# Moving an attention kernel's leftover rows into 64-partition tiles, with earlier casts and a later request for batch 2

## The chip, the cores and the metric

The kernel runs on one core of a Trainium2 chip. The metric is the device time of one execution in microseconds. Ratios between kernels are computed from the mean time of one kernel's fast runs over the mean of the other's fast runs in the same rounds on the same chip, with a 95% interval; they are therefore not quite the ratio of the medians that are quoted beside them. PE is the matmul engine and PEld its weight loads, DVE the vector engine, ACT the scalar engine, POOL the GpSimd engine, SP the engine that only issues transfers.

## The reference

Attention without softmax over 8 batches, 8 heads, 576 rows, head width 64; then a dense block of 512 to 2048 to 512 over all 4608 rows:

```python
kv  = einsum('bhsd,bhse->bhde', k, v)
out = einsum('bhsd,bhde->bhse', q, kv)
out = out / sqrt(mean(out*out, -1) + 1e-6) * g_norm
x   = out.transpose(0, 2, 1, 3).reshape(4608, 512)
h   = x @ w_in
y   = (h * sigmoid(1.702 * h)) @ w_out
```

576 rows are 512 + 64. The kernel treats the first 512 rows of each head as four blocks of 128 and the last 64 as "rests". The rests of all batches are gathered into a ninth tile of the dense block.

## The kernel before

Heads are handled in pairs. For each pair, `kv` accumulates four 128-row matmuls and one matmul over the rests into PSUM, `q` transposes the q blocks, `out` multiplies, and `ss` and `apply` do the normalization. The rests of heads 0 to 3 lie in partitions 0 to 63 and those of heads 4 to 7 in partitions 64 to 127 of the same tile. The v rests stand in a tile of zeros, so that a matmul over all 128 partitions picks the right half:

```python
def load_rest(dst, n, b, g, eng):          # g: heads 0..3 or 4..7
    eng.dma_start(out=dst, in_=srcs[n][b, 4*g : 4*g+4, SM:S, :].rearrange("h p d -> p h d"))
...
for c in range(NPAIR):                     # first batch: k, q f32 on SP; v and rests cast on POOL's queue
    load_rows(first["k"][:, h0:h1, :], "k", 0, h0, h1, nc.sync)
    load_rows(vh0[:, h0:h1, :], "v", 0, h0, h1, nc.gpsimd)
    load_rows(first["q"][:, h0:h1, :], "q", 0, h0, h1, nc.sync)
    if c % 2 == 0:
        first_rests(c // 2)
... # weights, batch 1 and batch 2, all on POOL's queue

def kv(self, c, alone):
    ...
    for j in range(J):                     # L214
        nc.tensor.matmul(o, self.kh[:, c, j, :], self.vh[...], start=(j == 0), stop=False)
    nc.tensor.matmul(                      # L221: 128 rows, half of them zeros in vr
        t[:, c, :], self.kr[:, c % 2, :], self.vr[:, c, :], start=False, stop=True
    )
    ...
def q(self, c):
    for j in range(J):                     # L235
        nc.tensor.transpose(t[:, j*P : (j+1)*P], self.qh[:, c, j, :], ident)
    if c >= 2:                             # L237: two transposes for four pairs
        nc.tensor.transpose(t[:, SM : SM+P], self.qr[:, c-2, :], ident)
    ...
a0 = Attention(0)
for c in range(NPAIR):                     # the first batch
    casts(0, [c], False)
    if c:
        a0.ss(c - 1)
    a0.kv(c, True)
    a0.q(c)
    a0.out(c)
    if c:
        a0.apply(c - 1)
```

The dense block of tile t (`hT` is the hidden matmul, L302; `o` the projection, L342) has the attention of batch t + 1 woven into it. For tile 0 that is done in the projection, pair by pair as data comes; from tile 1 on, kv and q of the next batch each follow one of the hidden groups.

Of the kernel before, what the change touches and what calls it, by code (L numbers as in the profile page):

```python
# [8 lines left out]
F16 = mybir.dt.float16  # L9
F32 = mybir.dt.float32  # L10
# [3 lines left out]
P = 128  # L14
# [3 lines left out]
def kernel(  # L18
# [45 lines left out]
            out=dst, in_=srcs[n][b, h0:h1, 0:SM, :].rearrange("h (p j) d -> p h (j d)", j=J)  # L64
        )

    def load_rest(dst, n, b, g, eng):
        eng.dma_start(out=dst, in_=srcs[n][b, 4 * g : 4 * g + 4, SM:S, :].rearrange("h p d -> p h d"))

    def load_batch(b, parts, eng):  # L70
        tiles = {}
        for n in "kvq":
            tiles[n] = stage.tile([P, H, J * D], F32, name=f"{n}f", tag=f"{n}f")
            tiles[n + "r"] = stage.tile([P, 4, D], F32, name=f"{n}rf", tag=f"{n}rf")
        step = H // parts
        for h0 in range(0, H, step):
            for n in "kvq":
                load_rows(tiles[n][:, h0 : h0 + step, :], n, b, h0, h0 + step, eng)
            if h0 == 0:
                for n in "kvq":  # L80
                    for g in range(2):
                        load_rest(tiles[n + "r"][g * R : (g + 1) * R], n, b, g, eng)
        staged[b] = tiles

    def new_halves(b):
        t = [half.tile([P, NPAIR, J, P], F16, name=f"{n}h", tag=f"{n}h") for n in "kq"]
        t.append(half.tile([P, H, J * D], F16, name="vh", tag="vh"))
        t += [half.tile([P, 2, P], F16, name=f"{n}r", tag=f"{n}r") for n in "kq"]
        halves[b] = (*t, vrem[b % 2])
        return halves[b]  # L90

    kvb = [const.tile([P, NPAIR, P], F16, name=f"kvb{i}") for i in range(2)]
    vrem = [const.tile([P, NPAIR, P], F16, name=f"vrem{i}") for i in range(2)]
    ident = const.tile([P, P], F16)
    ones2 = const.tile([P, P], F16)
    eps_t = const.tile([P, 1], F32)
# [3 lines left out]
    w_out_sb = const.tile([P, FO, DM], F16)  # L100
    x_rem = const.tile([P, KO, B * R], F16)

    nc.vector.memset(vrem[0], 0.0)
    nc.vector.memset(eps_t, EPS)
    for t in kvb:
        nc.vector.memset(t, 0.0)
    nc.vector.memset(ones2, 0.0)
    nc.vector.memset(ones2[0:D, 0:D], 1.0)
    nc.vector.memset(ones2[D:P, D:P], 1.0)
    nc.vector.memset(vrem[1], 0.0)  # L110
    for hl in range(2):
        nc.scalar.dma_start(out=g_col[hl * D : (hl + 1) * D, :], in_=g_norm.unsqueeze(1))
    nc.scalar.preload_act_table_set("natural_log_exp_and_others")


    kh0, qh0, vh0, kr0, qr0, vr0 = new_halves(0)
    first = {n: stage.tile([P, H, J * D], F32, name=f"{n}f", tag=f"{n}f") for n in "kq"}
    staged[0] = first

    def as_heads(t):  # L120
        return t.rearrange("p u (l d) -> p (u l) d", l=2)

    def first_rests(g):
        r = slice(g * R, (g + 1) * R)
        load_rest(as_heads(kr0)[r], "k", 0, g, nc.gpsimd)
        load_rest(as_heads(vr0)[r, 4 * g : 4 * g + 4], "v", 0, g, nc.gpsimd)

    for c in range(NPAIR):
        h0, h1 = 2 * c, 2 * c + 2
        load_rows(first["k"][:, h0:h1, :], "k", 0, h0, h1, nc.sync)  # L130
        load_rows(vh0[:, h0:h1, :], "v", 0, h0, h1, nc.gpsimd)
        load_rows(first["q"][:, h0:h1, :], "q", 0, h0, h1, nc.sync)
        if c % 2 == 0:
            first_rests(c // 2)
        if c == 0:
            make_identity(nc, ident)
    for g in range(2):
        load_rest(as_heads(qr0)[g * R : (g + 1) * R], "q", 0, g, nc.gpsimd)
    gate_t = const.tile([P, 1], F32)
    nc.gpsimd.tensor_copy(gate_t, first["q"][:, H - 3, 0:1])  # L140


    for i in range(4):
        nc.gpsimd.dma_start(
            out=w_in_sb[:, :, i * SM : (i + 1) * SM],
            in_=moe_w_in[:, i * SM : (i + 1) * SM].rearrange("(ko ki) f -> ki ko f", ki=P),
        )
    for i in range(4):
        nc.gpsimd.dma_start(
            out=w_out_sb[:, 4 * i : 4 * i + 4, :],  # L150
            in_=moe_w_out[4 * i * P : 4 * (i + 1) * P, :].rearrange(
                "(fo ki) n -> ki fo n", ki=P
            ),
        )
    load_batch(1, 4, nc.gpsimd)
    load_batch(2, 1, nc.gpsimd)


    def casts(b, pairs, rest):
        if b not in halves:  # L160
            new_halves(b)
        src = staged[b]
        kh, qh, vh, kr, qr, vr = halves[b]

        def pair(dst, s, c):
            return dict(
                out=dst[:, c, :, :].rearrange("p j (l d) -> p j l d", l=2),
                in_=s[:, 2 * c : 2 * c + 2, :].rearrange("p l (j d) -> p j l d", j=J),
            )

        for c in pairs:
            nc.vector.tensor_copy(**pair(kh, src["k"], c))  # L172
            if b == 0:
                nc.scalar.copy(**pair(qh, src["q"], c))
                continue
            nc.vector.tensor_copy(
                out=vh[:, 2 * c : 2 * c + 2, :], in_=src["v"][:, 2 * c : 2 * c + 2, :]
            )
            if c == pairs[0] and rest:
                nc.vector.tensor_copy(  # L180
                    out=kr, in_=src["kr"].rearrange("p (u l) d -> p u (l d)", l=2)
                )
                for g in range(2):
                    rows = slice(g * R, (g + 1) * R)
                    nc.vector.tensor_copy(
                        out=vr[rows, 2 * g : 2 * g + 2, :],
                        in_=src["vr"][rows].rearrange("p (u l) d -> p u (l d)", l=2),
                    )
                nc.vector.tensor_copy(
                    out=qr, in_=src["qr"].rearrange("p (u l) d -> p u (l d)", l=2)  # L190
                )
            nc.vector.tensor_copy(**pair(qh, src["q"], c))


    xT = {}
# [1 line left out]
    class Attention:  # L197
# [9 lines left out]
        def kv(self, c, alone):  # L207
# [5 lines left out]
            for j in range(J):  # L213
# [5 lines left out]
                    stop=False,  # L219
                )  # L220
            nc.tensor.matmul(  # L221
                t[:, c, :], self.kr[:, c % 2, :], self.vr[:, c, :], start=False, stop=True
            )
            cs = slice(c, c + 1) if alone else slice(0, NPAIR)
            if alone or c == NPAIR - 1:
                for hl in range(2):
                    r = slice(hl * D, (hl + 1) * D)
                    nc.vector.tensor_copy(self.kb[r, cs, r], t[r, cs, r])  # L228

        def q(self, c):  # L230
            n = SM + (P if c >= 2 else 0)
            pool, tag = (ps_h, "hT") if self.b < 2 else (ps_a, "att")
            t = pool.tile([P, SM + P], F16, name="qTp", tag=tag)
            for j in range(J):
                nc.tensor.transpose(t[:, j * P : (j + 1) * P], self.qh[:, c, j, :], ident)  # L235
            if c >= 2:
                nc.tensor.transpose(t[:, SM : SM + P], self.qr[:, c - 2, :], ident)  # L237
            s = attn.tile([P, SM + P], F16, name="qT", tag="qT")
            nc.vector.tensor_copy(s[:, 0:n], t[:, 0:n])  # L239
            self.qT[c] = s  # L240

        def out(self, c):
# [10 lines left out]
            else:  # L253
                n = NPAIR * R
                for i in range(NPAIR):
                    nc.tensor.matmul(
                        t.rearrange("p c r -> p (c r)")[:, i * R : (i + 1) * R],
                        self.kb[:, i, :],
                        self.qT[i | 2][:, SM + (i // 2) * R : SM + (i // 2 + 1) * R],
                        start=True,  # L260
                        stop=True,
                    )
# [113 lines left out]


    a0 = Attention(0)
    for c in range(NPAIR):
        casts(0, [c], False)  # L380
        if c:
            a0.ss(c - 1)
        a0.kv(c, True)
        a0.q(c)
        a0.out(c)
        if c:
            a0.apply(c - 1)
    a0.ss(NPAIR - 1)
    a0.apply(NPAIR - 1)

    live = {0: a0}

# [3 lines left out]
    for t in range(NT):  # L396
# [6 lines left out]
        def at2(i, f, *args):  # L403
            u2.setdefault(i, []).append(lambda: f(*args))
# [3 lines left out]

        if t < 2:
            at1(5, of(t, "out", NPAIR))  # L410
            at2(2, of(t, "ss", NPAIR, True))
            at2(2, of(t, "apply", NPAIR))
        if t == 0:
            new_halves(1)
            start(1)
            for c in range(NPAIR):
                s0 = 22 + 10 * c
                at2(s0, casts, 1, [c], c == 0)
                at2(min(s0 + 7, 63), of(1, "kv", c, True))
                at2(min(s0 + 9, 63), of(1, "q", c))  # L420
                if c < NPAIR - 1:
                    at2(s0 + 15, of(1, "out", c))
                    at2(s0 + 19, of(1, "ss", c))
                    at2(s0 + 19, of(1, "apply", c))
            at2(63, load_batch, 3, 1, nc.sync)
        elif b < B:
            at1(2, casts, b, list(range(NPAIR)), True)
            at1(2, start, b)
            for c in range(NPAIR):
                at1(8 + c, of(b, "kv", c, False))  # L430
# [5 lines left out]
            if b + 2 < B:  # L436
                at2(2, load_batch, b + 2, 1, nc.sync)
        if t == 1:
            at1(("ko", 1), of(1, "out", NPAIR - 1))
            at1(("ko", 2), of(1, "ss", NPAIR - 1))  # L440
            at1(("ko", 3), of(1, "apply", NPAIR - 1))
        dense(t, u1, u2, 4 if t < 2 else 0, t == 0)

# [29 lines left out]
```

## Time and profile before

| | before |
|---|---|
| median of the runs | 321.68 us (321.29 to 323.17) |
| span of the profiled run | 320.4 us |
| PE busy | 289.5 us |
| first hidden matmul | 28.56 us |
| one steady batch (start of its hidden matmuls to the next) | 31.81 us |

The page's engine totals and its row of 40 slices, for PE in the kernel before. A digit is the busy tenth of a slice of 8 us:

```profile
PE 289.5 (90%) x1560; PEld 139.7 (44%) x1560; DVE 112.4 (35%) x260; ACT 176.4 (55%) x284; POOL 32.7 (10%) x52
...
PE   0167999769899999999999999999999999999993
```

PE is full from the twelfth slice on. Only the first 88 us hold idle time. What ended it, from the list of PE's waits in the kernel before (total us, times, longest):

```profile
PE kvp L214 <- DMA vh<-in_v_dram: 8.6, 1, 8.6
PE kvp L221 <- DMA kr<-in_k_dram: 6.1, 1, 6.1
PE outT L245 <- DVE qT L239: 4.4, 6, 1.0
PE ss L273 <- ACT sq L265: 2.7, 4, 0.7
PE hT L302 <- DVE qT L239: 1.5, 1, 1.5
PE hT L302 <- DVE xT L283: 1.4, 1, 1.4
```

The first two lines are the start: 8.6 us to the first v pair, then 6.1 us to the k rests. The others are chains between engines in the attention of batches 0 and 1.

From there on the batches follow each other evenly.

### The profile page before, as it was taken

The numbers are of one execution on the slowest core, as the hardware profiler recorded it, in microseconds if no ns is written. First come the engines' busy times: TensorE is split into PE (matmuls) and PEld (weight loads), VectorE is DVE, ScalarE is ACT, GpSimd is POOL, SyncE is SP. The second block draws the span as 40 slices with busy tenths as digits, with TensorE's granted clock in tenths as the row PEclk, the third lists the DMA queues.
The fourth block names the chain that finished last, engine by engine and source line by source line (L and its number), as shares of the span: only waits on it lengthen the run. The fifth ranks groups of instructions, "written<-read, shape, count | busy, mean of one in ns | idle before, by whom it ended". The sixth has DMA issues, their size and how long they took to land.

```text
span 320.4 us, 3978 instructions
## 1 busy us (share of the span) xinstructions
PE 289.5 (90%) x1560; PEld 139.7 (44%) x1560; DVE 112.4 (35%) x260; ACT 176.4 (55%) x284; POOL 32.7 (10%) x52
## 2 busy tenths in 40 slices
PE   0167999769899999999999999999999999999993
PEld 0033445325444554455445544554455444444441
DVE  2053017654346334633462356225622520020021
ACT  2067762466775667566756675667567756206500
POOL 8552395000000000000000000000000000000000
PEclk9999999999999999999999999999999999999998
DMA  6999979599901770267026702000300030003022
GB/s 147 220 205 194 250 234 349 186 373 321 302 0 82 245 248 0 100 235 240 2 115 227 236 0 122 11 0 0 133 0 2 0 131 1 2 0 132 2 65 67
DMA packets 37012, 41.49 MB, mean 130 GB/s; under 512 B 11200, under 2 KB 33728, under 8 KB 35968
## 3 DMA queue, kind: packets, MB, share of 16 engines
q1 hardware_dynamic: 27728, 29.23, 27.2%
q0 software_dynamic: 9104, 12.00, 16.8%
q8 instruction: 12, 0.20, 0.2%
q14 instruction: 8, 0.07, 0.1%
q10 hardware_dynamic: 160, 0.00, 0.0%
HBM read 36.70 MB, written 9.44 MB: 144 GB/s over the span
## 4 chain that ended last, share of the span: by engine, by line
PE 87%; ACT 4%; DMA 3%; DVE 2%; issue 1%; POOL 1%; DVEq 0%; POOLq 0%
PE hT L302 38%; PE o L342 37%; DMA kr<-in_k_dram 3%; PE ss L273 3%; PE outT L245 3%; PE kvp L214 2%; PE qTp L235 2%; DVE qT L239 1%; ACT ln L275 1%; ACT rs L277 1%; ACT sq L265 1%; POOL vh L63 1%; PE kvp L221 1%; PE hO L302 0%; ACT L270 0%
## 5 line engine op out<-in xcount | busy, mean ns | idle before, releaser
L342 PE MATMUL o<-w_out_sb,gT 128*128 128x512 f16 x576 | 137.0, 379 | 0.0
L311 ACT ACTIVATE gT<-hT 128x512 f16<-128x512 f32 x142 | 84.4, 598 | 75.9 <-PE hT L302 75.7
L302 PE MATMUL hT<-xT,w_in_sb 128*128 128x512 f16 x504 | 119.7, 381 | 3.0 <-DVE qT L239 1.5
L342 PEld LDWEIGHTS <-gT 128*128 128x128 f16 x576 | 55.3, 98 | 66.7 <-issue 5.4
L302 PEld LDWEIGHTS <-w_in_sb 128*128 128x128 f16 x576 | 54.8, 98 | 63.4 <-issue 7.2
L350 DVE COPY osb<-o 128x512 f32<-128x512 f32 x36 | 24.7, 685 | 62.1 <-PE o L342 62.1
L283 DVE SCALAR_TENSOR_TENSOR xT<-outT,g_col,rs 128x512 f16<-128x512 f32 x32 | 24.0, 750 | 50.0 <-ACT rs L277 50.0
L265 ACT ACTIVATE sq<-outT 128x512 f16<-128x512 f32 (+1 forms) x40 | 21.7, 544 | 27.3 <-PE outT L245 27.3
L275 ACT ACTIVATE ln<-ss,eps_t 128x512 f32<-128x512 f32 (+1 forms) x40 | 25.8, 645 | 17.1 <-PE ss L273 17.0
L228 DVE CAST kvb<-kvp 64x64 f16<-64x64 f32 (+1 forms) x28 | 8.6, 307 | 50.2 <-PE kvp L221 50.0
L277 ACT ACTIVATE rs<-ln 128x512 f32<-128x512 f32 (+1 forms) x40 | 23.5, 587 | 1.3
L214 PE MATMUL kvp<-vh,kh 128*128 128x128 f16 x128 | 13.3, 231 | 8.6 <-DMA vh<-in_v_dram 8.6
L239 DVE COPY qT<-qTp 128x512 f16<-128x512 f16 (+1 forms) x32 | 14.6, 457 | 13.8 <-PE qTp L237 8.2
L214 PEld LDWEIGHTS <-kh 128*128 128x128 f16 x128 | 10.3, 102 | 19.7 <-DVE kh L172 7.7
L273 PE MATMUL ss<-sq,ones 128*128 128x512 f16 (+1 forms) x40 | 15.1, 378 | 3.6 <-ACT sq L265 2.7
L245 PE MATMUL outT<-qT,kvb 128*128 128x512 f16 x32 | 12.9, 404 | 4.6 <-DVE qT L239 4.4
L172 DVE CAST kh<-kf 128x512 f16<-128x512 f32 x32 | 13.7, 429 | 1.1 <-DMA kf<-in_k_dram 1.1
L302 PE MATMUL hT<-x_rem,w_in_sb 128*128 128x512 f16 x64 | 14.0, 379 | 0.0
L235 PE MATMUL qTp<-ident,qh 128*128 128x128 f16 x128 | 13.4, 231 | 0.0
L235 PEld LDWEIGHTS <-qh 128*128 128x128 f16 x128 | 10.4, 104 | 6.6
L221 PE MATMUL kvp<-vrem,kr 128*128 128x128 f16 x32 | 7.3, 229 | 6.1 <-DMA kr<-in_k_dram 6.1
L287 DVE SCALAR_TENSOR_TENSOR x_rem<-outT,g_col,rs 128x256 f16<-128x256 f32 x8 | 3.9, 483 | 25.0 <-ACT rs L277 25.0
(44 smaller groups left out, 114.5 us busy)
## 6 DMA issues: line engine op xcount, KB each, us to landing
out_dram<-osb SPq DMA_DIRECT2D x8, 1024.0 KB, 3.8
kf<-in_k_dram SPq DMA_DIRECT2D x5, 1024.0 KB, 5.9
vf<-in_v_dram SPq DMA_DIRECT2D x5, 1024.0 KB, 8.5
qf<-in_q_dram SPq DMA_DIRECT2D x5, 1024.0 KB, 11.2
w_in_sb<-in_moe_w_in_dram POOLq DMA_DIRECT2D x4, 512.0 KB, 8.8
w_out_sb<-in_moe_w_out_dram POOLq DMA_DIRECT2D x4, 512.0 KB, 16.7
kf<-in_k_dram SPq DMA_DIRECT2D x4, 256.0 KB, 7.9
qf<-in_q_dram SPq DMA_DIRECT2D x4, 256.0 KB, 8.7
```

Source lines behind the costliest of these rows:

```text
L214: nc.tensor.matmul(o, self.kh[:, c, j, :], self.vh[:, 2 * c : 2 * c + 2, j * D : (j + 1) * D], start=(j == 0), stop=False,)
L235: nc.tensor.transpose(t[:, j * P : (j + 1) * P], self.qh[:, c, j, :], ident)
L245: nc.tensor.matmul(t.rearrange("p c r -> p (c r)"), self.kb[:, c, :], self.qT[c][:, 0:SM], start=True, stop=True,)
L265: nc.scalar.activation(sq[:, 0:n], t, AFT.Square)
L273: nc.tensor.matmul(t[:, 0:n], ones2, sq[:, 0:n], start=True, stop=True)
L275: nc.scalar.activation(ln[:, 0:n], t[:, 0:n], AFT.Ln, bias=eps_t, scale=1.0 / D)
L277: nc.scalar.activation(rs[:, 0:n], ln[:, 0:n], AFT.Exp, bias=0.0, scale=-0.5)
L283: nc.vector.scalar_tensor_tensor(self.x[:, c, :], o, g_col, rs, op0=ALU.mult, op1=ALU.mult)
L302: nc.tensor.matmul(h, w_in_sb[:, ko, fo * P : (fo + 1) * P], x[:, ko, :], start=(ko == 0), stop=(ko == KO - 1),)
L311: nc.scalar.activation(gT[:, fo, :], h, AFT.Gelu_apprx_sigmoid)
L342: nc.tensor.matmul(os[mo], gT[:, fo, mo * P : (mo + 1) * P], w_out_sb[:, fo, :], start=(fo == 0), stop=(fo == FO - 1),)
L350: nc.vector.tensor_copy(osb[:, mo, :], os[mo])
```

## The change

It moves all eight heads' rests of a tensor into one tile of 64 partitions, in one transfer in place of two. The zero-filled v tile goes, and so does the contraction over its zeros. First-batch v is no longer cast by the transfer. Casts run one pair ahead and are spread over DVE, ACT and POOL. Batch 1's attention is spread differently over the first projection, and batch 2 is requested on SP's queue once batch 1's third q pair is in. For batches 0 and 1 one multiplication by a mask replaces the two copies of `kv`. The diff, cut to its core:

```diff
-    def load_rest(dst, n, b, g, eng):
-        eng.dma_start(out=dst, in_=srcs[n][b, 4 * g : 4 * g + 4, SM:S, :].rearrange("h p d -> p h d"))
+    def load_rest(dst, n, b, eng):
+        eng.dma_start(out=dst, in_=srcs[n][b, :, SM:S, :].rearrange("h p d -> p h d"))
...
-        t += [half.tile([P, 2, P], F16, name=f"{n}r", tag=f"{n}r") for n in "kq"]
-        halves[b] = (*t, vrem[b % 2])
+        t += [half.tile([R, NPAIR, P], F16, name=f"{n}r", tag=f"{n}r") for n in "kqv"]
+        halves[b] = t
... (first batch: rests first on POOL's queue, then k, v, q pair by pair on SP's)
         for c in pairs:
+            h = slice(2 * c, 2 * c + 2)
             nc.vector.tensor_copy(**pair(kh, src["k"], c))
+            eng = nc.vector if b > 1 else nc.gpsimd
+            eng.tensor_copy(out=vh[:, h, :], in_=src["v"][:, h, :])
+            if b > 1 or (b == 0 and c % 2):
+                nc.vector.tensor_copy(**pair(qh, src["q"], c))
+            else:
                 nc.scalar.copy(**pair(qh, src["q"], c))
+    def cast_rests(b):
+        for n, t in (("kr", kr), ("vr", vr), ("qr", qr)):
+            nc.gpsimd.tensor_copy(out=t.rearrange("p c (l d) -> p (c l) d", l=2), in_=src[n])
...
             nc.tensor.matmul(
-                t[:, c, :], self.kr[:, c % 2, :], self.vr[:, c, :], start=False, stop=True
+                t[:, c, :], self.kr[:, c, :], self.vr[:, c, :], start=False, stop=True
             )
...
-            if c >= 2:
-                nc.tensor.transpose(t[:, SM : SM + P], self.qr[:, c - 2, :], ident)
+            nc.tensor.transpose(t[:, SM:S], self.qr[:, c, :], ident[0:R, 0:R])
...
+    casts(0, [0])
     for c in range(NPAIR):
-        casts(0, [c], False)
+        a0.kv(c, True)
+        a0.q(c)
         if c:
             a0.ss(c - 1)
-        a0.kv(c, True)
-        a0.q(c)
+        if c + 1 < NPAIR:
+            casts(0, [c + 1])
         a0.out(c)
...
+    def load_third():
+        nc.scalar.copy(after, staged[1]["q"][:, H - 3, 0:1])
+        nc.sync.dma_start(out=after[0:D, :], in_=g_norm.unsqueeze(1))
+        load_batch(2, 1, nc.sync)
...
-                s0 = 22 + 10 * c
-                at2(s0, casts, 1, [c], c == 0)
+                s0 = 30 + 7 * c
+                at2(s0, casts, 1, [c])
```

More of the change, by code (lines that the diff above doesn't have):

```diff
@@ L73, in load_batch @@
             tiles[n] = stage.tile([P, H, J * D], F32, name=f"{n}f", tag=f"{n}f")
-            tiles[n + "r"] = stage.tile([P, 4, D], F32, name=f"{n}rf", tag=f"{n}rf")
+            tiles[n + "r"] = stage.tile([R, H, D], F32, name=f"{n}rf", tag=f"{n}rf")
         step = H // parts
@@ L80, in load_batch @@
                 for n in "kvq":
-                    for g in range(2):
-                        load_rest(tiles[n + "r"][g * R : (g + 1) * R], n, b, g, eng)
+                    load_rest(tiles[n + "r"], n, b, eng)
         staged[b] = tiles
@@ L87, in new_halves @@
         t.append(half.tile([P, H, J * D], F16, name="vh", tag="vh"))
-        t += [half.tile([P, 2, P], F16, name=f"{n}r", tag=f"{n}r") for n in "kq"]
-        halves[b] = (*t, vrem[b % 2])
+        t += [half.tile([R, NPAIR, P], F16, name=f"{n}r", tag=f"{n}r") for n in "kqv"]
+        halves[b] = t
         return halves[b]
     kvb = [const.tile([P, NPAIR, P], F16, name=f"kvb{i}") for i in range(2)]
-    vrem = [const.tile([P, NPAIR, P], F16, name=f"vrem{i}") for i in range(2)]
     ident = const.tile([P, P], F16)
@@ L101 @@
     x_rem = const.tile([P, KO, B * R], F16)
-    nc.vector.memset(vrem[0], 0.0)
     nc.vector.memset(eps_t, EPS)
@@ L109, with load_w_in @@
     nc.vector.memset(ones2[D:P, D:P], 1.0)
-    nc.vector.memset(vrem[1], 0.0)
-    for hl in range(2):
-        nc.scalar.dma_start(out=g_col[hl * D : (hl + 1) * D, :], in_=g_norm.unsqueeze(1))
-    nc.scalar.preload_act_table_set("natural_log_exp_and_others")
-    kh0, qh0, vh0, kr0, qr0, vr0 = new_halves(0)
-    first = {n: stage.tile([P, H, J * D], F32, name=f"{n}f", tag=f"{n}f") for n in "kq"}
-    staged[0] = first
-    def as_heads(t):
-        return t.rearrange("p u (l d) -> p (u l) d", l=2)
-    def first_rests(g):
-        r = slice(g * R, (g + 1) * R)
-        load_rest(as_heads(kr0)[r], "k", 0, g, nc.gpsimd)
-        load_rest(as_heads(vr0)[r, 4 * g : 4 * g + 4], "v", 0, g, nc.gpsimd)
+    nc.scalar.preload_act_table_set("natural_log_exp_and_others")
+    first = {n: stage.tile([P, H, J * D], F32, name=f"{n}f", tag=f"{n}f") for n in "kvq"}
+    staged[0] = first
+    _, _, _, kr0, qr0, vr0 = new_halves(0)
+    for n, t in (("k", kr0), ("v", vr0), ("q", qr0)):
+        load_rest(t.rearrange("p c (l d) -> p (c l) d", l=2), n, 0, nc.gpsimd)
+    make_identity(nc, ident)
+    for hl in range(2):
+        nc.gpsimd.dma_start(out=g_col[hl * D : (hl + 1) * D, :], in_=g_norm.unsqueeze(1))
     for c in range(NPAIR):
         h0, h1 = 2 * c, 2 * c + 2
-        load_rows(first["k"][:, h0:h1, :], "k", 0, h0, h1, nc.sync)
-        load_rows(vh0[:, h0:h1, :], "v", 0, h0, h1, nc.gpsimd)
-        load_rows(first["q"][:, h0:h1, :], "q", 0, h0, h1, nc.sync)
-        if c % 2 == 0:
-            first_rests(c // 2)
-        if c == 0:
-            make_identity(nc, ident)
-    for g in range(2):
-        load_rest(as_heads(qr0)[g * R : (g + 1) * R], "q", 0, g, nc.gpsimd)
-    gate_t = const.tile([P, 1], F32)
-    nc.gpsimd.tensor_copy(gate_t, first["q"][:, H - 3, 0:1])
-    for i in range(4):
+        for n in "kvq":
+            load_rows(first[n][:, h0:h1, :], n, 0, h0, h1, nc.sync)
+    def load_w_in(i):
         nc.gpsimd.dma_start(
@@ L147, with load_w_out @@
         )
-    for i in range(4):
+    def load_w_out(i):
         nc.gpsimd.dma_start(
@@ L154, with casts @@
         )
-    load_batch(1, 4, nc.gpsimd)
-    load_batch(2, 1, nc.gpsimd)
-    def casts(b, pairs, rest):
+    def casts(b, pairs):
         if b not in halves:
@@ L171, in casts @@
         for c in pairs:
+            h = slice(2 * c, 2 * c + 2)
             nc.vector.tensor_copy(**pair(kh, src["k"], c))
-            if b == 0:
-                nc.scalar.copy(**pair(qh, src["q"], c))
-                continue
-            nc.vector.tensor_copy(
-                out=vh[:, 2 * c : 2 * c + 2, :], in_=src["v"][:, 2 * c : 2 * c + 2, :]
-            )
-            if c == pairs[0] and rest:
-                nc.vector.tensor_copy(
-                    out=kr, in_=src["kr"].rearrange("p (u l) d -> p u (l d)", l=2)
-                )
-                for g in range(2):
-                    rows = slice(g * R, (g + 1) * R)
-                    nc.vector.tensor_copy(
-                        out=vr[rows, 2 * g : 2 * g + 2, :],
-                        in_=src["vr"][rows].rearrange("p (u l) d -> p u (l d)", l=2),
-                    )
-                nc.vector.tensor_copy(
-                    out=qr, in_=src["qr"].rearrange("p (u l) d -> p u (l d)", l=2)
-                )
-            nc.vector.tensor_copy(**pair(qh, src["q"], c))
+            eng = nc.vector if b > 1 else nc.gpsimd
[3 more added lines that the diff above has]
+            else:
+                nc.scalar.copy(**pair(qh, src["q"], c))
+    def cast_rests(b):
+        src = staged[b]
+        _, _, _, kr, qr, vr = halves[b]
+        for n, t in (("kr", kr), ("vr", vr), ("qr", qr)):
+            nc.gpsimd.tensor_copy(out=t.rearrange("p c (l d) -> p (c l) d", l=2), in_=src[n])
     xT = {}
@@ L221, in kv @@
             nc.tensor.matmul(
-                t[:, c, :], self.kr[:, c % 2, :], self.vr[:, c, :], start=False, stop=True
+                t[:, c, :], self.kr[:, c, :], self.vr[:, c, :], start=False, stop=True
             )
-            cs = slice(c, c + 1) if alone else slice(0, NPAIR)
-            if alone or c == NPAIR - 1:
+            if alone:
+                nc.vector.tensor_mul(self.kb[:, c, :], t[:, c, :], ones2)
+            elif c == NPAIR - 1:
                 for hl in range(2):
                     r = slice(hl * D, (hl + 1) * D)
-                    nc.vector.tensor_copy(self.kb[r, cs, r], t[r, cs, r])
+                    nc.vector.tensor_copy(self.kb[r, :, r], t[r, :, r])
         def q(self, c):
-            n = SM + (P if c >= 2 else 0)
             pool, tag = (ps_h, "hT") if self.b < 2 else (ps_a, "att")
-            t = pool.tile([P, SM + P], F16, name="qTp", tag=tag)
+            t = pool.tile([P, S], F16, name="qTp", tag=tag)
             for j in range(J):
                 nc.tensor.transpose(t[:, j * P : (j + 1) * P], self.qh[:, c, j, :], ident)
-            if c >= 2:
-                nc.tensor.transpose(t[:, SM : SM + P], self.qr[:, c - 2, :], ident)
-            s = attn.tile([P, SM + P], F16, name="qT", tag="qT")
-            nc.vector.tensor_copy(s[:, 0:n], t[:, 0:n])
+            nc.tensor.transpose(t[:, SM:S], self.qr[:, c, :], ident[0:R, 0:R])
+            s = attn.tile([P, S], F16, name="qT", tag="qT", bufs=5)
+            nc.vector.tensor_copy(s, t)
             self.qT[c] = s
@@ L258, in out @@
                         self.kb[:, i, :],
-                        self.qT[i | 2][:, SM + (i // 2) * R : SM + (i // 2 + 1) * R],
+                        self.qT[i][:, SM:S],
                         start=True,
@@ L378 @@
     a0 = Attention(0)
+    casts(0, [0])
     for c in range(NPAIR):
-        casts(0, [c], False)
+        a0.kv(c, True)
+        a0.q(c)
         if c:
             a0.ss(c - 1)
-        a0.kv(c, True)
-        a0.q(c)
+        if c + 1 < NPAIR:
+            casts(0, [c + 1])
+        if c == 1:
+            load_w_in(0)
         a0.out(c)
@@ L389 @@
     a0.apply(NPAIR - 1)
+    for i in range(1, 4):
+        load_w_in(i)
+    for i in range(4):
+        load_w_out(i)
+    load_batch(1, 4, nc.gpsimd)
+    after = const.tile([P, 1], F32)
+    def load_third():
+        nc.scalar.copy(after, staged[1]["q"][:, H - 3, 0:1])
+        nc.sync.dma_start(out=after[0:D, :], in_=g_norm.unsqueeze(1))
+        load_batch(2, 1, nc.sync)
     live = {0: a0}
@@ L410 @@
             at1(5, of(t, "out", NPAIR))
-            at2(2, of(t, "ss", NPAIR, True))
-            at2(2, of(t, "apply", NPAIR))
+            at2(5, of(t, "ss", NPAIR, True))
+            at2(5, of(t, "apply", NPAIR))
         if t == 0:
@@ L416 @@
             for c in range(NPAIR):
-                s0 = 22 + 10 * c
-                at2(s0, casts, 1, [c], c == 0)
-                at2(min(s0 + 7, 63), of(1, "kv", c, True))
-                at2(min(s0 + 9, 63), of(1, "q", c))
+                s0 = 30 + 7 * c
+                at2(s0, casts, 1, [c])
+                if c == 2:
+                    at2(s0, load_third)
+                if c == 0:
+                    at2(s0, cast_rests, 1)
+                at2(s0 + 5, of(1, "kv", c, True))
+                at2(s0 + 6, of(1, "q", c))
+                at2(s0 + 12, of(1, "out", c))
                 if c < NPAIR - 1:
-                    at2(s0 + 15, of(1, "out", c))
-                    at2(s0 + 19, of(1, "ss", c))
-                    at2(s0 + 19, of(1, "apply", c))
+                    at2(s0 + 17, of(1, "ss", c))
+                    at2(s0 + 17, of(1, "apply", c))
             at2(63, load_batch, 3, 1, nc.sync)
         elif b < B:
-            at1(2, casts, b, list(range(NPAIR)), True)
+            at1(2, casts, b, list(range(NPAIR)))
+            at1(2, cast_rests, b)
             at1(2, start, b)
@@ L438 @@
         if t == 1:
-            at1(("ko", 1), of(1, "out", NPAIR - 1))
-            at1(("ko", 2), of(1, "ss", NPAIR - 1))
+            at1(("ko", 1), of(1, "ss", NPAIR - 1))
             at1(("ko", 3), of(1, "apply", NPAIR - 1))
```

## The prediction

> **What bounds it now.** PE is busy 289.5 of 320.4 us (page part 1); the windows show it full from about 88 us on, so only the first 88 us can give time: some 25 us of idle PE. By PE's waits and the timeline: 8.6 us until the first v pair, then 6.1 until the second half of k's rest rows (landed 15.2); then four first-batch pairs, one per 3.45 us, PE half idle, until the first dense matmul at 28.56; then about 5 us of waits on DVE/ACT between 57 and 70 us (batch 1's attention inside the first projection), and 0.85 us at 86 behind a table load.
>
> **Costs, step by step.**
> 1. Start. The rests go first on the software queue, in 3 transfers for 6, and v leaves it. But they are still 1,536 small cast packets, and pair 0's transposes now need qr, the last. Before, the software queue moved 200 to 240 packets/us beside the hardware queue (per-microsecond DMA view at 7 to 9 us), began at 4.0 us, and landed about 1.7 us after its last packet. My estimate: kr lands near 8, vr 10, qr 12 us, against 15.2 for kr. The Trainium skill ("DMA: Bandwidth & Descriptors", Queues, rings and completion order) says engines round-robin between queues per packet; the counts at 8 to 9 us (268 and 236) agree. Gain 2.5 us.
> 2. Pairs. Casts leave the path, kvb's two 230 ns copies become one multiply, the apply goes later on DVE. What stays is ACT's loop, sq to ss to ln to rs: 17.13 to 19.75 us, 2.6 us, plus one 0.6 us q cast in one turn. Three turns fall from 3.45 to about 2.85: gain 1.7, and 0.7 on pair 0's own chain. POOL's v cast is off this path: none is in the trace; an estimate of 0.8 to 0.9 us from "GPSIMD Engine Reference" (3.1: 512 elements in 769 ns). First dense matmul at 24 to 25 us.
> 3. Weights. The same bytes are read, 2.55 us per weight quarter; w_in's first quarter goes out at about 14 us and lands before 20: no stall. Batch 1 still lands behind them, at 40 to 48 us, before its casts at step 30 (about 46 us).
> 4. Batch 1's attention. DVE per pair falls from 2.9 to 1.9 us (v cast to POOL, q cast to ACT), ACT rises to 2.5, just the pair's PE time. The 5 us of waits fall to 1 to 1.5 (the last ss and apply chain): gain 3.5 us.
> 5. Batch 2, requested at about 50 us on the SP queue, needs 14 us (batch 3 before: 61.7 to 76), just before its kv matmuls at 65. Risk 0 to 2 us.
> 6. Rest transposes: 4 of 64 columns for 2 of 128; 64-column matmuls ran at 29 ns (four in 0.12 us), 128-column ones at 54: nothing. The table wait stays. Steady batches unchanged at 31.8 us.
>
> **Prediction.** 321.7 - 2.5 - 1.7 - 0.7 - 3.5 = 313.3 us, range 307.5 to 318. Chances: faster by over 2% 0.68, within 2% 0.30, slower 0.02.
>
> **Right or wrong is shown by:** PE's wait before the first kvp and qTp matmuls, and on which rest tile; the start of the first hidden matmul; PE's waits between 50 and 70 us; whether batches from 88 us keep 31.8 us.
>
> **What would make it wrong:** rests landing much sooner (9 us: 310) or as late as before; POOL casts blocked by DVE copies, delaying weights; batch 1 or 2 late, turning the removed waits into DMA waits.

## More of the kernel before

The chain of work that ended last, in order of time (start, duration), shows where the hidden matmuls of two successive tiles begin in the kernel before:

```profile
101.02 7.77 PE hT L302 x36
...
132.83 7.77 PE hT L302 x36
```

Their distance, 31.81 us, is one steady batch. Inside it, this is how one pair's kv stands between hidden groups of four in the kernel before (timeline: start, duration, engine, line, operation, weight rows * columns, shape, count; ends of matmuls are modelled, so read the starts):

```profile
140.44 0.39 PE L214 MATMUL kvp<-vh,kh 128*128 128x128 f16 x4
140.66 0.22 PE L221 MATMUL kvp<-vrem,kr 128*128 128x128 f16 x1
140.72 1.03 PE L302 MATMUL hT<-xT,w_in_sb 128*128 128x512 f16 x4
141.58 0.39 PE L214 MATMUL kvp<-vh,kh 128*128 128x128 f16 x4
```

Four kv matmuls start within 0.22 us, the rest matmul L221 takes 0.06 us until the next hidden group starts, and one such slot lasts 1.14 us (140.44 to 141.58). The weight loads of the same stretch, kernel before:

```profile
140.22 0.43 PEld L214 LDWEIGHTS <-kh 128*128 128x128 f16 x4
140.61 0.10 PEld L221 LDWEIGHTS <-kr 128*128 128x128 f16 x1
140.66 0.58 PEld L302 LDWEIGHTS <-w_in_sb 128*128 128x128 f16 x4
```

The loads of `kr` (140.61) and of the next `w_in_sb` (140.66) start about 0.05 us before their own matmuls (140.66 and 140.72), beside the matmul ahead of them: they are hidden.

## The result, and the profile after

| | before | after |
|---|---|---|
| median of the runs | 321.68 us | 325.29 us (324.96 to 325.67) |
| span of the profiled run | 320.4 us | 323.2 us |
| PE busy | 289.5 us | 302.8 us |
| first hidden matmul | 28.56 us | 22.71 us |
| one steady batch | 31.81 us | 33.48 us |

The ratio is 1.0104 (1.0069 to 1.0139): about 1% slower, clear of noise but less than 2%, where 2.6% faster was predicted. The same two rows of the page, kernel after:

```profile
PE 302.8 (94%) x1576; PEld 142.2 (44%) x1576; DVE 103.9 (32%) x216; ACT 176.9 (55%) x287; POOL 38.3 (12%) x63
...
PE   0579999899999999999999999999999999999993
```

PE gained 13.3 us of busy time although the change adds almost no arithmetic. And it is full sooner. PE's waits, kernel after:

```profile
PE kvp L188 <- POOL vh L156: 5.9, 1, 5.9
PE kvp L195 <- DMA vr<-in_v_dram: 2.8, 1, 2.8
PE ss L246 <- ACT sq L238: 1.5, 2, 1.1
PE qTp L210 <- DMA qr<-in_q_dram: 1.3, 1, 1.3
...
PE outT L218 <- DVE qT L212: 0.8, 2, 0.5
```

The start behaved as hoped: 5.9 us to the first v cast where it was 8.6, then 2.8 for the v rests and 1.3 for the q rests where it was 6.1. The waits of batches 0 and 1 have shrunk. So the first part gained. The rest gave it back, as the chain of the kernel after shows:

```profile
95.50 7.77 PE hT L275 x36
...
128.98 7.77 PE hT L275 x36
```

The tile whose hidden matmuls began at 101.02 us now begins 5.52 us sooner, but the next follows after 33.48 us in place of 31.81. Five batches remain to be woven in from that point; 5 x 1.67 - 5.52 = 2.8 us, which is the difference of the two spans. Here is one slot inside such a batch, kernel after:

```profile
137.94 0.39 PE L188 MATMUL kvp<-vh,kh 128*128 128x128 f16 x4
138.26 0.23 PE L195 MATMUL kvp<-vr,kr 64*128 64x128 f16 x1
138.42 1.04 PE L275 MATMUL hT<-xT,w_in_sb 128*128 128x512 f16 x4
139.29 0.39 PE L188 MATMUL kvp<-vh,kh 128*128 128x128 f16 x4
```

and its weight loads, kernel after:

```profile
137.73 0.43 PEld L188 LDWEIGHTS <-kh 128*128 128x128 f16 x4
138.26 0.09 PEld L195 LDWEIGHTS <-kr 64*128 64x128 f16 x1
138.41 0.55 PEld L275 LDWEIGHTS <-w_in_sb 128*128 128x128 f16 x4
```

The slot lasts 1.35 us in place of 1.14. The rest matmul, now marked 64*128, starts 0.32 us after the first kv matmul in place of 0.22, and the next hidden group 0.16 us after it in place of 0.06. Neither its own weight load nor that of the next `w_in_sb` starts ahead any more: each begins with its own matmul. That makes about 0.10 us on the way in and 0.10 on the way out. A batch has four such kv slots and four q slots (1.33 us where a q slot without a rest took 1.09 and one with a 128-row rest 1.14): 4 x 0.21 + 2 x 0.18 + 2 x 0.24 = 1.68 us, the whole growth of the batch.

### The profile page after: what moved, and what is told of

It reads as the page before. It is cut to its first block, busy times and chain, and to the rows that moved or that the text cites. A ratio compares the mean times of both kernels' runs of the same rounds, so it can differ in the third digit from the quotient of the medians.

```text
span 323.2 us, 3990 instructions
## 1 busy us (share of the span) xinstructions
PE 302.8 (94%) x1576; PEld 142.2 (44%) x1576; DVE 103.9 (32%) x216; ACT 176.9 (55%) x287; POOL 38.3 (12%) x63
## 4 chain that ended last, share of the span: by engine, by line
PE 81%; DMA 12%; ACT 3%; POOL 2%; issue 1%; DVE 0%; SPq 0%
PE o L315 36%; PE hT L275 35%; DMA qf<-in_q_dram 7%; DMA w_in_sb<-in_moe_w_in_dram 3%; PE ss L246 2%; DMA vf<-in_v_dram 2%; PE kvp L188 2%; PE qTp L209 2%; PE outT L218 2%; PE kvp L195 1%; PE qTp L210 1%; ACT ln L248 1%; ACT rs L250 1%; POOL vf L63 0%; POOL qf L63 0%
## 5 line engine op out<-in xcount | busy, mean ns | idle before, releaser
L275 PEld LDWEIGHTS <-w_in_sb 128*128 128x128 f16 x576 | 53.1, 98 | 64.2 <-issue 5.7
L212 DVE COPY qT<-qTp 128x576 f16<-128x576 f16 x32 | 14.6, 457 | 21.8 <-PE qTp L210 21.8
L188 PE MATMUL kvp<-vh,kh 128*128 128x128 f16 x128 | 13.3, 230 | 6.3 <-POOL vh L156 5.9
L166 POOL CAST kr<-krf 64x512 f16<-64x512 f32 x7 | 4.4, 626 | 121.1 <-PE hT L275 53.0
L203 DVE CAST kvb<-kvp 64x256 f16<-64x256 f32 x12 | 5.1, 422 | 40.3 <-PE kvp L195 40.2
L154 DVE CAST kh<-kf 128x512 f16<-128x512 f32 x32 | 15.1, 471 | 1.7 <-DMA kf<-in_k_dram 1.7
L209 PE MATMUL qTp<-ident,qh 128*128 128x128 f16 x128 | 13.3, 230 | 0.7 <-ACT qh L160 0.7
L158 DVE CAST qh<-qf 128x512 f16<-128x512 f32 x26 | 12.0, 461 | 2.1 <-DMA qf<-in_q_dram 2.1
```

The lines of the kernel that those rows point to most:

```text
L188: nc.tensor.matmul(o, self.kh[:, c, j, :], self.vh[:, 2 * c : 2 * c + 2, j * D : (j + 1) * D], start=(j == 0), stop=False,)
L209: nc.tensor.transpose(t[:, j * P : (j + 1) * P], self.qh[:, c, j, :], ident)
L275: nc.tensor.matmul(h, w_in_sb[:, ko, fo * P : (fo + 1) * P], x[:, ko, :], start=(ko == 0), stop=(ko == KO - 1),)
```

## The experiments

**Theory A.** Each 64-row matmul (or transpose) that stands between 128-row ones, called one visit below, costs PE about 0.2 us. The Trainium skill has something near this in "TensorEngine Tiling (Array Packing)", Tiling Modes, Key Properties: "Mode switching requires drain: Changing tiling mode (not just tile) drains the TensorE". It names no size, and that one 64-row matmul is such a change of mode is my reading, not the page's words. **Rival B**: the batches are longer because of what runs beside them, the rest casts on POOL or transfers. **Rival C**: it is the four narrow transposes in place of two.

### full, kvfull, qfull: the rests again 128 rows deep, inside the changed kernel

Edit (for q; the same for k and v, and kvfull or qfull have only their part): tiles of 128 partitions, two per tensor, whose lower half is set to zero once.

```diff
+    rests = {n: [const.tile([P, NPAIR, P], F16, name=f"{n}r{i}") for i in range(2)] for n in WIDE}
+        nc.vector.memset(rests[n][0][R:P], 0.0)      # and [1]
-            nc.tensor.transpose(t[:, SM:S], self.qr[:, c, :], ident[0:R, 0:R])
+            nc.tensor.transpose(t[:, SM : SM + P], self.qr[:, c, :], ident)
```

> The changed kernel with k, q and v rests kept in 128-partition tiles whose lower 64 rows are zero, so that every rest matmul and transpose has 128 rows as the others do. Theory A (each 64-row matmul between 128-row ones costs PE about 0.2 us, in draining and in a weight load that is no longer hidden): a steady batch falls from 33.48 to about 31.9 us, and the time from 325.3 to about 314 us, below both kernels. Rival B (the steady batches are longer because of the rest casts on POOL, or of DMA): the batch stays at 33.4 us and the time at 325.

> Only the kv rests (k and v) in zero-padded 128 rows, the q rests still 64. A: four visits of 0.21 us less in a batch, 33.48 to about 32.65 us, time about 319.5. B: no change. Rival C (it is the four narrow 64-column rest transposes in place of two that cost): no change, 33.4 us, as the kv rests have 128 columns in both.

> Only the q rests in zero-padded 128 rows, their four transposes 128 columns wide. A: four visits of about 0.18 us less in a batch, 33.48 to about 32.75 us, time about 320. B: no change. C (four transposes in place of two): at most a little, as there are still four.

| | median us | ratio to before (95%) | steady batch us |
|---|---|---|---|
| after | 325.29 | 1.0104 (1.0069 to 1.0139) | 33.48 |
| kvfull | 321.31 | 0.9966 (0.9928 to 1.0004) | 32.65 |
| qfull | 321.28 | 0.9960 (0.9922 to 0.9997) | 32.75 |
| full | 314.75 | 0.9770 (0.9730 to 0.9811) | 31.92 |
| before | 322.24 in these rounds | | 31.81 |

Each half gives its half and together they give all: 0.83 and 0.73 us of the batch, 1.56 for both, as A said to within 0.1 us. The chain of full shows two successive tiles:

```profile
94.99 7.77 PE hT L281 x36
...
126.91 7.77 PE hT L281 x36
```

B falls: the POOL casts and the transfers are all still there in full, and the batch is 31.92 us. C falls too: qfull and full still have four rest transposes, even twice as wide. The last 0.11 us over the batch before fit the two extra 128-column transposes, at 0.055 us each. In time, kvfull and qfull came out 1 to 2 us slower than I had expected, because the first 90 us moved as well: the tile that begins at 95.50 us in the changed kernel begins at 97.32 in kvfull and 95.75 in qfull. In both, PE waited for POOL's casts of batch 1 (1.18 and 0.72 us in kvfull, 1.62 and 0.72 in qfull; 0.27 in the changed kernel), and the granted clock then stood at 0.50 for a while (50 to 52 us and 48 to 50 us). The run fullact below takes up this wait.

### before64: the same narrowing, alone, in the kernel before

```diff
+            g = slice(0, R) if c < 2 else slice(0, P)
             nc.tensor.matmul(
-                t[:, c, :], self.kr[:, c % 2, :], self.vr[:, c, :], start=False, stop=True
+                t[:, c, :], self.kr[g, c % 2, :], self.vr[g, c, :], start=False, stop=True
             )
```

(Pairs 2 and 3 have their rests in partitions 64 to 127. Narrowing these too is not among the runs: the check before the chip refuses it, because matmuls from two row positions would then write one PSUM bank unordered. Its message calls these matmuls "tiling mode 64x128".)

> The kernel before, with nothing changed but that the kv rest matmuls of pairs 0 and 1 contract the 64 rows that hold data and not the 64 rows of zeros below them. Less work by count. A: two visits of 0.21 us more in a batch, 31.81 to about 32.2 us, time from 321.7 to about 324.7. B and C: unchanged at 321.7 or a little less.

Measured: 321.17 us, ratio 0.9964 (0.9946 to 0.9983), so the time missed the expectation. The batch did not: 32.22 us. The edit had a second effect that I had overlooked. With rows 0 to 63 alone, pairs 0 and 1 of the first batch no longer wait for the second half of the k rests, and the first hidden matmul came at 24.10 us in place of 28.56. The next two runs separate the two effects.

### steady64 and first64: the two effects apart

```diff
-            g = slice(0, R) if c < 2 else slice(0, P)
+            g = slice(0, R) if self.b > 1 and c < 2 else slice(0, P)     # steady64
+            g = slice(0, R) if self.b == 0 and c < 2 else slice(0, P)    # first64
```

> The run before64 changed two things: it narrowed matmuls, and it let pairs 0 and 1 of the first batch go without the second half of k's rests. Here the kernel before narrows only the batches from the third on (pairs 0 and 1), where nothing waits for data. If each 64-row visit costs 0.21 us of PE: a batch 32.23 in place of 31.81 us, six of them, the time 2.5 us above before (ratio about 1.008). If the visit is free and the earlier trace misled: unchanged.

> The other half of before64: only the first batch's pairs 0 and 1 contract 64 rows, so that they wait for the first half of the rests alone. If that false wait was what before64 gained: PE's wait for k rests of 6.1 us falls below 2, the first hidden matmul comes 4 to 5 us before 28.56, the batches stay at 31.81, and the time falls by 3.5 to 4.5 us to about 318. If the gain came from somewhere else, the time is that of before.

steady64 took 324.41 us, ratio 1.0083 (1.0056 to 1.0109), with a batch of 32.22 us. Two slots of its timeline, the first with a 64-row rest, the second with a 128-row one, in one kernel and one trace:

```profile
142.35 0.39 PE L214 MATMUL kvp<-vh,kh 128*128 128x128 f16 x4
142.67 0.23 PE L222 MATMUL kvp<-vrem,kr 64*128 64x128 f16 x1
142.83 1.04 PE L303 MATMUL hT<-xT,w_in_sb 128*128 128x512 f16 x4
143.70 0.39 PE L214 MATMUL kvp<-vh,kh 128*128 128x128 f16 x4
143.93 0.22 PE L222 MATMUL kvp<-vrem,kr 128*128 128x128 f16 x1
143.98 1.03 PE L303 MATMUL hT<-xT,w_in_sb 128*128 128x512 f16 x4
```

From the first kv matmul to the next hidden group it is 0.48 us with the 64-row rest and 0.28 with the 128-row one, which multiplies twice as many rows, half of them by zeros. This is theory A with nothing else of the change present.

first64 took 318.48 us, ratio 0.9893 (0.9865 to 0.9921), with a batch of 31.81 us and the first hidden matmul at 24.39. Its wait at the rest matmul, where the kernel before has 6.1 us:

```profile
PE kvp L222 <- DMA vrem<-in_v_dram: 1.6, 1, 1.6
```

So the same narrowing wins 3.3 us on two matmuls of the first batch, where a wait goes, and loses 2.6 on twelve later ones, where none does.

### grouped: one visit in place of four

The changed kernel, with the four kv rest matmuls of a batch (from the third batch on) one after the other ahead of the 128-row ones, as one accumulation group in the bank:

```diff
+            if not alone and c == 0:
+                for i in range(NPAIR):
+                    rest(i, start=(i == 0), stop=False, skip_group_check=True)
             for j in range(J):
                 nc.tensor.matmul(o, self.kh[:, c, j, :], self.vh[...],
-                    start=(j == 0), stop=False)
+                    start=(alone and j == 0), stop=(not alone and j == J - 1 and c == NPAIR - 1), ...)
+            if alone:
+                rest(c, start=False, stop=True)
```

> The changed kernel with the four 64-row kv rest matmuls of each batch from the third on done one after the other, ahead of the 128-row ones: one visit for four, with the same instructions in number and shape. If what costs is the change between 64-row and 128-row matmuls: 3 x 0.21 = 0.63 us less in a batch (33.48 to about 32.85), six batches, about 3.8 us less than the changed kernel (321.5). If each 64-row matmul pays on its own, whatever stands beside it: no change (325).

Measured: 321.20 us, ratio 0.9977 (0.9954 to 1.0001), batch 32.86 us. The instructions of a steady batch are the same in number and shape as in the changed kernel; three visits fewer are worth 0.62 us. Its timeline, where the four rests stand together:

```profile
135.54 0.40 PE L189 MATMUL kvp<-vr,kr 64*128 64x128 f16 x4
135.87 0.40 PE L195 MATMUL kvp<-vh,kh 128*128 128x128 f16 x4
136.11 1.03 PE L282 MATMUL hT<-xT,w_in_sb 128*128 128x512 f16 x4
```

Four 64-row rests take 0.33 us from first start to the next matmul, little more than twice what one alone took (0.16). What costs is the change between 64-row and 128-row work, not the 64-row matmul. Whether PE spends the time draining, or only on a weight load that no longer starts ahead, these runs do not separate: the load of `kr` takes 0.09 us, about what is lost on each way.

### fullact: what full still waited for

In full, POOL's timeline and then PE's in the same stretch:

```profile
45.20 0.71 POOL L63 DMA_DIRECT2D qf<-in_q_dram  x1
45.90 0.62 POOL L162 CAST vh<-vf 128x512 f16<-128x512 f32 x1
...
47.02 0.61 POOL L172 CAST vr<-vrf 64x512 f16<-64x512 f32 x1
```

```profile
46.58 0.38 PE L194 MATMUL kvp<-vh,kh 128*128 128x128 f16 x4 [1.70 <-POOL vh L162]
47.68 0.22 PE L201 MATMUL kvp<-vr,kr 128*128 128x128 f16 x1 [0.72 <-POOL vr L172]
...
48.30 2.40 PE L321 MATMUL o<-w_out_sb,gT 128*128 128x512 f16 x6
```

POOL took its instructions in program order, and batch 1's casts stand behind the issue of batch 1's transfers, several of which wait for an earlier landing. The first v cast came at 45.90 us, and PE waited 1.70 and 0.72 us. After that, six projection matmuls took 2.40 us, 0.40 us each in place of 0.22; the slow stretch lasted until about 52 us, and the granted clock was 0.50 between 50 and 52 us. The Trainium skill ("TensorE: Matmul & The Clock Gate", Why this matters for your kernels) warns that an idle gap of more than about 3 us drops the matmul clock to half; here 2.4 us of waiting in 2.8 us came before it. The edit moves batch 1's first v cast and its rest casts to ACT, which was idle there:

```diff
+            if b == 1 and c == 0:
+                nc.scalar.copy(out=vh[:, h, :], in_=src["v"][:, h, :])
+            else: ...
-            nc.gpsimd.tensor_copy(out=t[0:R]..., in_=src[n])
+            cast = nc.scalar.copy if b == 1 else nc.gpsimd.tensor_copy
+            cast(out=t[0:R]..., in_=src[n])
```

> The run full with batch 1's first v cast and its rest casts on ACT in place of POOL. In full, PE waited 1.7 us for the v cast and 0.7 for the v rests at 45 to 48 us, POOL being busy issuing batch 1's transfers until 45.9; and then four microseconds of matmuls took 0.43 us each in place of 0.216. If POOL's order is the cause: these waits and the slow matmuls go, 2.4 to 4 us, time about 311 to 312. If the rows themselves were late: the wait turns into one for a DMA, and the time stays at 314.7.

Measured: 312.57 us, ratio 0.9706 (0.9665 to 0.9747), the fastest version. PE's timeline in fullact has no wait left at that place, and the matmuls that follow are at 0.22 us. The trace shows this more surely than the times show the gain: the medians of full and fullact are 2.2 us apart, their intervals overlap a little, and the two profiles are of full's slowest run (316.57 us) and fullact's fastest (310.81).

```profile
43.43 0.39 PE L198 MATMUL kvp<-vh,kh 128*128 128x128 f16 x4
...
44.20 1.46 PE L325 MATMUL o<-w_out_sb,gT 128*128 128x512 f16 x6
```

The runs of full and fullact spread over 3 us (fullact 310.81 to 313.78), more than the kernel before. Part of it may be how fast the first hidden matmuls run: in fullact's profiled run (span 309.0 us) they took 0.22 us each, in all the other profiles listed here about 0.43. What decides this from run to run was not tested, and the clock record does not settle it: the granted clock was 0.50 from 18 to 24 us in full, but 1.00 from 20 to 24 us in the changed kernel, whose matmuls there took 0.43 us too.

### nogate and noahead: two parts of the change by themselves, taken out of fullact

The gate is the copy and the small transfer that hold the request for batch 2 back until batch 1's third q pair has landed. nogate takes them out:

```diff
-        nc.scalar.copy(after, staged[1]["q"][:, H - 3, 0:1])            # nogate
-        nc.sync.dma_start(out=after[0:D, :], in_=g_norm.unsqueeze(1))
```

> The run fullact without the gate: batch 2 goes out on the SP queue as soon as its buffers are free (about 19 us), in the middle of the weights and ahead of batch 1. If the two queues share the engines evenly, the 7 MB of weights then still to come slow down until batch 2's 3.4 MB are in; w_out's last quarter and batch 1 land some 8 to 10 us later (weights' end near 47 in place of 38 us, batch 1 after 50), PE waits for them in the first projection, and the time rises from 312.6 by 5 to 10 us. If the gate is worth nothing: 312.6.

Measured: 325.74 us, ratio 1.0106 (1.0053 to 1.0159): 13 us slower than fullact, more than the 5 to 10 expected. Among PE's waits is one that fullact does not have, and POOL's issues show the pace of the weights, each waiting for one more quarter of a weight matrix to land:

```profile
PE o L325 <- DMA w_out_sb<-in_moe_w_out_dram: 4.9, 3, 3.3
```

```profile
37.79 0.68 POOL L68 DMA_DIRECT2D qrf<-in_q_dram  x1 [3.58 <-DMA w_out_sb<-in_moe_w_out_dram]
42.07 0.71 POOL L63 DMA_DIRECT2D kf<-in_k_dram  x1 [3.60 <-DMA w_out_sb<-in_moe_w_out_dram]
```

These two issues are 4.28 us apart; the same two in fullact, at 31.96 and 35.22 us, 3.26. Over the six quarters between the first v and the second v transfer of batch 1 it is 4.2 us a quarter in nogate (21.04 to 46.38 us) and 2.7 in fullact (21.74 to 37.82). Holding batch 2 back is worth a great deal. The wait for `w_out_sb` is 4.9 us of the loss; slow matmuls followed it (16 in 5.82 us, 0.36 each), and the rest was not traced.

noahead puts the first batch's casts back at the head of each turn, and the ss before the kv (the load of `w_in`'s first quarter moves along, so that it still follows the third pair's casts):

```diff
-    casts(0, [0])
     for c in range(NPAIR):
+        casts(0, [c])
+        if c: a0.ss(c - 1)
         a0.kv(c, True)
         a0.q(c)
-        if c: a0.ss(c - 1)
-        if c + 1 < NPAIR: casts(0, [c + 1])
```

> The run fullact with the first batch's casts back at the head of each turn and the ss before the kv, as in the kernel before. If casting a pair ahead is what shortened the turns from 3.45 to about 2.85 us: sq to sq is 3.3 to 3.5 us again, the first hidden matmul comes about 1.7 us later, and the time is about 314.3. If ACT's loop bounds the turns in either order: no change.

Measured: 315.63 us, ratio 0.9805 (0.9784 to 0.9827), 3.1 us slower than fullact. ACT's squares in noahead:

```profile
13.50 0.60 ACT L248 ACTIVATE sq<-outT 128x512 f16<-128x512 f32 x1 [5.53 <-PE outT L228]
...
23.91 0.60 ACT L248 ACTIVATE sq<-outT 128x512 f16<-128x512 f32 x1 [0.85 <-PE outT L228]
```

With those at 16.97 and 20.44 us between them, they are 3.47 us apart each time; in fullact they begin at 12.23, 15.49, 18.08 and 20.58 us. The new order of the loop, casting ahead and the later ss together, saves 2.1 us over the three turns, a little more than the 1.7 expected. The other 1.3 us lie before the first square, where PE waited 3.4 us for the v rests in noahead and 2.1 in fullact. That is a difference of landing between two executions, so I do not count it for the order of the loop.

## Why the prediction was wrong

The step that failed is number 6: "Rest transposes: 4 of 64 columns for 2 of 128 ... nothing", together with "Steady batches unchanged at 31.8 us". I priced the narrower instructions by their columns, with 64-column matmuls of 29 ns that I had read from the trace. Those had 128 rows of weights. I did not ask what 64 *rows* do, and I did not price the kv rest matmul at all, as its columns had not changed. The page of the skill that names the drain at a change of mode was there to be read. Shown: kvfull, qfull and full remove it by halves and whole; steady64 produces it in the kernel before; grouped shows that it is paid per change of form. A batch grows by 1.67 us where nothing was forecast, and 1.56 of it goes when the rests are padded. The six batches from the third on pay it in full, about 10 us; what batches 0 and 1 pay was not measured apart.

The other steps, point by point:

- **Start.** k, v and q rests let PE go on at 7.43, 9.27 and 11.39 us (weight load of kr, first rest matmul, first rest transpose of the timeline after); the estimate was 8, 10 and 12. Right.
- **Pairs.** ACT's squares began at 12.79, 16.44, 19.20 and 21.70 us, turns of 3.65, 2.76 and 2.50 us, 2.97 in the mean where 2.85 was estimated. From the first square to the last it is 8.91 us where the kernel before took 10.40: a gain of 1.5, with 1.7 forecast. The first square itself came 4.34 us sooner, where steps 1 and 2 had 2.5 + 0.7. So the first hidden matmul came at 22.71 us, better than 24 to 25. noahead shows, in the padded kernel, that the order of the loop is worth 2.1 us there.
- **Weights and batch 1.** No wait of PE for w_in, w_out or batch 1's rows in the kernel after. Right. The casts that I had called off the path on POOL were not quite: they stood behind POOL's own issue of transfers. In the kernel after that cost PE 0.3 us; in full, which came to that point sooner, 2.4 us and a slow stretch. I had listed POOL's casts as a risk, but for another reason.
- **Batch 1's attention.** The waits between 57 and 70 us fell from about 5 to between 1 and 2 us. Right.
- **Batch 2.** Requested at 51.2 us; no wait of PE for it. nogate shows that the gate is worth 13 us.
- **Sum.** Without step 6 the forecast was right in kind: full came to 314.75 us and, with POOL's order mended, fullact to 312.57, where 313.3 was forecast. That fullact lies so near is in part luck, as it holds a repair that the forecast did not have. The change holds a gain of about 7 us (full against before) and a loss of about 10.5 (after against full).

## What to carry to other kernels

Price a matmul by the form of its weights too. A matmul with 64 rows among neighbours with 128 cost a change of form here on the way in and on the way out, about 0.1 us each, so pad it with zeros to the neighbours' form or put all of its kind together; a tile half full of zeros can be the faster one. Where an engine both issues transfers and computes, its computation can stand behind its issues, as POOL's casts of batch 1 did. An experiment that narrows an operand also changes what it waits for: run the two effects apart.

## What the Trainium skill lacked or had wrong

- "TensorEngine Tiling (Array Packing)", Key Properties: says that a change of tiling mode drains the engine, but neither its size nor that a lone 64-row matmul among 128-row ones is such a change. The runs show 0.21 us per visit (kv rest, 128 columns) over the same matmul padded to 128 rows.
- "TensorE: Matmul & The Clock Gate", Why this matters for your kernels, the rule for small-K matmuls, says that a single matmul over 32 rows takes the time of one over 128; it leaves out what a change of rows costs. No run here has 32 rows. Four 64-row matmuls in a row took the 0.40 us of four 128-row ones (run grouped), but with a lone 64-row rest the next group starts 0.48 us after the first kv matmul, with a 128-row one 0.28.
- "TensorE: Matmul & The Clock Gate", Back-to-back issue gap, gives 131 ns as the sustained pace of 512-column matmuls, each with its weight load; here 36 of them in a row took 7.77 us, 216 ns each.
- The same page, Why this matters for your kernels, warns of idle gaps of more than about 3 us. Here shorter ones came before a granted clock of 0.50: waits of 1.70 and 0.72 us in full, 1.18 and 0.72 in kvfull. In full four microseconds followed at 0.40 to 0.43 us per 512-column matmul; fullact, without the waits, has no such stretch there.
- "GPSIMD Engine Reference", 3.1, has 769 ns for 512 elements as the best case; POOL's casts of 128x512 from float32 to float16 took 0.61 us when nothing disturbed them (spans on POOL are rough).
